# Integer phases, smaller first loads and other filler matmuls in the opening of an FFT and GeGLU kernel

## The chip, the cores and the metric

The kernel runs on one core of a Trainium2 chip. A core has five engines that run side by side, each with its own instruction queue: PE (matrix products, with PEld, its weight loads), DVE (vector work), ACT (activation functions and copies), POOL (general work) and SP, which here only issues DMA transfers. They meet through semaphores. The metric is the device time of one execution in microseconds; the median of a few runs counts.

## The reference

The input `x` has 8 batches of 3008 rows of 256 numbers. It is transformed by a Fourier transform along the rows and another along the columns, the real part is kept, and every one of the 24064 rows then goes through a gated feed-forward block with 1536 hidden units:

```
X = np.fft.fft(x, axis=1); X = np.fft.fft(X, axis=2); y = X.real
g = y @ w_gate;  gelu = 0.5 * g * (1 + erf(g / sqrt(2)))
out = (gelu * (y @ w_val)) @ w_out
```

All inputs and the output are fp32.

## The kernel before

The transform along the 3008 rows is split as 64 times 47. **Stage one** is the 64-point part: the rows of one batch are loaded into three tiles `xin` (8 rows of 256 for each of 128 partitions, line 201 `load_x`), folded into sums and differences of mirrored columns (`fold_x`, line 218; the two columns that have no partner are copied by `singles` on POOL), and multiplied by a table `G` of cosines and sines. For batch 0 this is done by `a_group` (line 513) in six groups J of four rows each: 16 small matmuls per group, copied from PSUM into the tile `S1`, and written from there by a DMA into the tile `Ap`, which has another order of partitions. **Stage two** is the 47-point part (`b_steps`, line 560): matmuls with `Ap` as weights and small tables `TP`, `TQ`, `T0P`, `T0Q`. The column transform is multiplied into the gate and value weights once (`gen_w`, with the table `CW`). What follows, the feed-forward block of all 8 batches in units of 512 columns, with the transforms of the next batch mixed in by a written plan, is nearly all of the time and is not edited.

The tables are made on the chip. `phase_g` (line 330) makes phases of `G` as products of a row number and a column number, for the first eight rows on DVE, for the next eight as eight ACT copies; adds a quarter turn for the cosines; and takes off whole turns with `reduce_phase`: two DVE operations, adding and subtracting a large constant `MAGIC` to round. `sin_g` then takes the sine on ACT, once for each sign of a column `col_h`, and `turn_g` derives eight more rows. `phase_c`, `reduce_c` and `sin_c` do the same for `CW`; `phase_t` and `sin_t` for the small tables, with `cols_t` and `quats` making columns for them.

The order on each engine is that of the program: every call is kept in program order, and the engines wait for one another only through the semaphores that the framework places from the tiles. DMAs are issued by SP in order, and each takes one of eight completion semaphores in turn ("lanes"); a DMA on a lane whose earlier user has not been seen to complete waits for it first. `warm(n)` (line 867) issues n matmuls of 512 columns whose result nobody reads: fillers. Their numbers are `WF = (10, 4)`: ten ahead of the first `gen_w` calls and four behind them, right before stage two; two more stand after the second group. In the profile nearly every instruction has line 25, a helper that records it, so tiles are what tells them apart; the tiles `dv` and `ev` hold the phases, since they share memory with later tiles of those names.

The part of the program around the change, before:

```
    for i in range(3):
        for a0, n in ((0, 8),) if i < 2 else ((0, 4), (4, 4)):
            fold_x(0, i, vec, a0, n, single=False)
    ...
    for J in range(6):
        a_group(J)
        if J == 1:
            warm(2)
    reduce_c()
    pt = phase_t()
    warm(WF[0])
```

Of the kernel before, what the change touches and what calls it, by code (L numbers as in the profile page):

```python
# [8 lines left out]

FP32 = mybir.dt.float32  # L10
BF16 = mybir.dt.bfloat16
AF = mybir.ActivationFunctionType
ALU = mybir.AluOpType

MAGIC = 12582912.0
TWO_PI = 2.0 * math.pi
# [11 lines left out]
def _sub(base: bass.AP, free_pattern, free_offset, part_start=0, part_num=None):  # L28
    p_step, p_count = base.ap[0]
    if part_num is None:  # L30
        part_num = p_count - part_start
    pat = [[p_step, part_num]] + [list(x) for x in free_pattern]
    off = base.offset + part_start * p_step + free_offset
    return ap_replace(base, ap=pat, offset=off)
# [3 lines left out]
def kernel(  # L38
# [24 lines left out]
    B, T, C = x.shape  # L63
# [27 lines left out]
    CW = const_pool.tile([128, NCH, 2, 128], BF16)  # L91
# [19 lines left out]
    col_a = const_pool.tile([128, 1], FP32)  # L111
    col_f = const_pool.tile([128, 1], FP32)
    col_b = const_pool.tile([128, 1], FP32)
    col_c = const_pool.tile([128, 1], FP32)
    col_j = const_pool.tile([128, 1], FP32)
    prow = const_pool.tile([1, 641], BF16)
    cols = const_pool.tile([128, 5], FP32)
# [58 lines left out]
    def apart(log, half, inst):  # L176
        for other, h in log:
            if half is not None and h is not None and h != half:
                tc.declare_no_dep(
                    getattr(inst, "ins", inst), getattr(other, "ins", other),  # L180
                    reason="the two halves of the tile are two banks")
        log.append((inst, half))
        return inst
# [16 lines left out]

    def load_x(b, i):
        xt = xins[i]
        for o, n, nh in ([(0, 7, 2), (7, 1, 1)] if i == 2 else [(0, 8, 2)]):
            src = ap_replace(
                x, ap=[[N2 * C, N1], [HJ * C, nh], [1, n * C]],
                offset=x.offset + (b * T + 8 * i + o) * C)
            p_step = xt[:, :, :].ap[0][0]
            dst = ap_replace(
                xt[:, :, :], ap=[[p_step * 2 // nh, N1 * nh], [1, n * C]],
                offset=xt[:, :, :].offset + o * C)  # L210
            sync.dma_start(out=dst, in_=src)
# [6 lines left out]
    def fold_x(b, i, eng, a0=0, an=8, single=True):  # L218
        xt = xins[i]
        o0 = (8 * i + a0) * C  # L220
        lo = _sub(xt, [[C, an], [1, 127]], a0 * C + 1)
        hi = _sub(xt, [[C, an], [-1, 127]], a0 * C + 255)
        ea = _sub(xf, [[C, an], [1, 127]], o0 + 1)
        od = _sub(xf, [[C, an], [1, 127]], o0 + 129)
        eng.tensor_tensor(ea, lo, hi, op=ALU.add)
        eng.tensor_tensor(od, lo, hi, op=ALU.subtract)
        if single:
            singles(i, a0, an)
# [10 lines left out]
    iota(rowj, [[15, HJ]], 0, 0)  # L239
    iota(_sub(rowk, [[1, 33]], 0), [[1, 33]], 0, 0)  # L240
    iota(_sub(rowk, [[1, 31]], 33), [[1, 31]], 1, 0)
    pool.tensor_scalar(rowk, rowk, 1.0 / 64.0, None, op0=ALU.mult)

    iota(_sub(rowc, [[128, 2], [1, 128]], 0), [[0, 2], [1, 128]], 0, 0)
    pool.memset(_sub(rowc, [[1, 1]], 128), 128.0)
# [25 lines left out]
    TG = TO + 2 * NJ  # L271

    def rows_t():
        pool.tensor_scalar(col_c, col_p, 1.0 / C, None, op0=ALU.mult)
        iota(_sub(rowt, [[N2, 2], [1, N2]], 0), [[0, 2], [1, N2]], 0, 0)
        iota(_sub(rowt, [[NJ, 2], [1, MID]], TO), [[0, 2], [1, MID]], 0, 0)
        iota(_sub(rowt, [[NJ, 2], [1, MID - 1]], TO + MID), [[0, 2], [1, MID - 1]], 1, 0)
        pool.memset(_sub(rowt, [[NJ, 2]], TO + NJ - 1), 0.0)
        pool.memset(_sub(quat, [[1, NJ]], TO), 0.25)
        pool.memset(_sub(quat, [[1, NJ]], TO + NJ), 0.0)  # L280
        iota(_sub(rowt, [[NG, 2], [1, NG]], TG), [[0, 2], [-11, NG]], 0, 0)
        pool.memset(_sub(quat, [[1, NG]], TG), 0.25)
        pool.memset(_sub(quat, [[1, NG]], TG + NG), 0.5)
# [28 lines left out]
    vec.scalar_tensor_tensor(col_a, col_f, -719.0, col_a, op0=ALU.mult, op1=ALU.add)  # L312
    vec.tensor_scalar(rowj, rowj, col_a, None, op0=ALU.add)
    vec.scalar_tensor_tensor(col_b, col_f, -2.0, col_p, op0=ALU.mult, op1=ALU.add)
    vec.tensor_scalar(col_h[1], col_b, -TWO_PI, None, op0=ALU.mult)
    vec.tensor_scalar(col_h[0], col_b, TWO_PI, -TWO_PI, op0=ALU.mult, op1=ALU.add)

    def reduce_phase(ph, tmp):
        vec.tensor_scalar(tmp, ph, MAGIC, None, op0=ALU.add)
        vec.scalar_tensor_tensor(tmp, tmp, MAGIC, ph, op0=ALU.subtract, op1=ALU.subtract)  # L320

    def red2_tile():
        return work.tile([128, 512], FP32, tag="glm", bufs=3, name="red2")
# [4 lines left out]
    reds = []  # L328

    def phase_g(i):  # L330
        ph, red = pha_g[i // 2][:, i % 2, :], red_g[i // 2][:, i % 2, :]
        reds.append(red)
        if i == 0:
            vec.tensor_tensor(
                _sub(ph, [[64, 8], [1, 64]], 0), _sub(rowj, [[1, 8], [0, 64]], 0),
                _sub(rowk, [[0, 8], [1, 64]], 0), op=ALU.mult)
        else:
            for k in range(8):
                act.activation(ph[:, 64 * k : 64 * k + 64], rowk[:, :], AF.Copy,
                               scale=rowj[:, 8 * i + k : 8 * i + k + 1])  # L340
        cos = _sub(ph, [[64, 8], [1, 33]], 0)
        vec.tensor_scalar(cos, cos, 0.25, None, op0=ALU.add)
        reduce_phase(ph, red)

    def sin_g(i):
        for h in range(2):
            act.activation(
                _sub(G, [[128, 8], [1, 64]], i * 8 * 128 + h * 64),
                _sub(reds[i], [[64, 8], [1, 64]], 0), AF.Sin, scale=col_h[h][:, :])

    def turn_g(odd):
        for to, of, n, sign in (((1, 33, 8, 1.0), (33, 1, 8, -1.0), (3, 35, 8, -1.0), (35, 3, 8, 1.0))
# [29 lines left out]
    redc = []  # L382

    def phase_c():
        both = red2_tile()
        redc.append(both)
        for q, (o, n) in enumerate(((0, 129), (129, 127))):
            act.activation(both[:, o : o + n], rowc[:, o : o + n], AF.Copy, scale=col_c[:, :],
                           bias=0.25 * (q + 1))

    def reduce_c():
        reduce_phase(redc[0][:, :C], redc[0][:, C : 2 * C])

    def sin_c():
        act.activation(_sub(CW, [[1, C]], 0), redc[0][:, C : 2 * C], AF.Sin, scale=-TWO_PI)
        for o, sign in ((0, 1.0), (1, -1.0)):
            act.activation(_sub(CW, [[2, 128]], C + o), _sub(CW, [[2, 128]], o), AF.Copy, scale=sign)

# [114 lines left out]
    def a_group(J):  # L513
        if "S1" not in st[0]:
            st[0]["S1"] = S1_tile()
        S1 = st[0]["S1"]
        if J % 4 < 2:
            ps, log = ps_v(), []
            both = ps
            banks = [(ps[:, h, :], log) for h in range(2)]  # L520
        else:
            banks = [(f(), []) for f in ((ps_g, ps_g) if J % 4 == 2 else (ps_o, ps_d))]
        for gq in range(4):
            for jl in range(4):
                jj = 4 * J + jl
                ps, log = banks[gq // 2]
                apart(log, gq // 2, pe.matmul(
                    _sub(ps, [[1, C]], gq % 2 * C, 32 * jl, 32),
                    _sub(G, [[32, 4], [4, 8]], (jj - 16 * (J > 3 and gq % 2 == 0)) * 128 + gq),
                    _sub(xf, [[1, C]], jj * C), start=True, stop=True))  # L530
        if J > 3:
            for o, n, scale in ((0, 2, 1.0), (2, 1, -1.0), (3, 1, 1.0)):
                ps, log = banks[o // 2]
                to, of = _sub(S1, [[1, n * C]], (4 * J + o) * C), _sub(ps, [[1, n * C]], o % 2 * C)
                apart(log, o // 2, vec.tensor_scalar(to, of, scale, None, op0=ALU.mult) if J == 4 and o else
                      act.activation(to, of, AF.Copy, scale=scale))
        if J < 2:
            act.activation(_sub(S1, [[1, 4 * C]], 4 * J * C), both, AF.Copy)
        for h in range(2 * (J in (2, 3))):
            dst = _sub(S1, [[1, 2 * C]], (4 * J + 2 * h) * C)  # L540
            act.activation(dst, banks[h][0], AF.Copy)
        p_step = Ap[:, :, :].ap[0][0]
        sync.dma_start(
            out=ap_replace(
                Ap[:, :, :], ap=[[6 * p_step, 16], [1, NG * C]],
                offset=Ap[:, :, :].offset + (J % 2 * 3 + J // 2) * p_step),
            in_=_sub(S1, [[1, 4 * C]], 4 * J * C))
# [314 lines left out]
        return steps  # L862


    WF = (10, 4)

    def warm(n, w=None):
        ps = ps_d()
# [8 lines left out]
    sin_g(0)  # L877
    sin_g(1)
    turn_g(True)
    phase_c()  # L880
    for i in range(3):
        for a0, n in ((0, 8),) if i < 2 else ((0, 4), (4, 4)):
            fold_x(0, i, vec, a0, n, single=False)
        if i == 0:
            singles(0)
            cols_t()
            singles(1)
            quats()
            singles(2)
    for J in range(6):  # L890
        a_group(J)
        if J == 1:
            warm(2)
    reduce_c()
    pt = phase_t()
    warm(WF[0])
    for f0, n in ((256, 256), (512, 512)):
        for i in (1, 0):
# [206 lines left out]
```

## Time and profile before

| | us |
|---|---|
| median of 3 runs (lowest, highest) | 615.92 (615.8, 619.26) |
| the profiled execution's own time | 616.09 |
| its span, first to last instruction | 614.2 |
| PE busy | 595.6 (97%) |
| DVE busy | 567.1 (92%) |
| POOL busy | 501.7 (82%) |
| ACT busy | 487.2 (79%) |
| first matmul of stage one | 8.97 |
| last copy into `S1` ends | 16.03 |
| first matmul of stage two | 21.08 |

Times inside a run count from the span's first instruction. A timeline line gives the start, the length from the first to the last of the merged instructions, engine, line, operation, what it writes and reads, the size, how many, and in brackets how long the engine was idle before it and who ended that. A line of waits gives who waited for whom, then total, times and longest. A line of the chain gives start, length and what the end of the run was waiting for at that moment, followed back from the last instruction.

### The profile page before, as it was taken

Reading aid. Unit: us, or ns where it says so; the run is one execution under the profiler, and the core shown is the slowest. Engines: PE = TensorE matmul, PEld = TensorE weight load, DVE = VectorE, ACT = ScalarE, POOL = GpSimd, SP = SyncE. Lnnn points to the kernel's source line nnn. Section 1 sums busy time; section 2 is a strip of 40 time slices with the busy share of each in tenths; the row PEclk is TensorE's granted clock in tenths of the full one; section 3 lists DMA queues with packets and bytes.
Section 4 is the critical chain, followed back from the end, with each engine's and each line's share of the span. In section 5 each row is a group of like instructions: output and inputs, shape, how many; then the busy total and the mean of one; then the engine's idle time right before and its main releaser. Section 6 shows DMA issues by size and latency. Waiting matters only on the chain.

```text
span 614.2 us, 13086 instructions
## 1 busy us (share of the span) xinstructions
PE 595.6 (97%) x4572; PEld 398.5 (65%) x4629; DVE 567.1 (92%) x689; ACT 487.2 (79%) x1011; POOL 501.7 (82%) x525
## 2 busy tenths in 40 slices
PE   4899999999999999999999999999999999999997
PEld 2456666666676666666667666766667666666666
DVE  8688999999999999999999999999999999999992
ACT  8798789877898787977789778887789878776762
POOL 5599999989999899798998899898997755665552
PEclk9999999999999999999999999999999999999999
DMA  7999423762257613673246633477123712222123
GB/s 277 340 241 268 132 69 112 204 215 60 61 149 196 197 40 80 193 225 113 65 120 172 194 92 74 121 207 214 41 73 94 203 37 55 55 47 52 39 48 87
DMA packets 63460, 80.79 MB, mean 132 GB/s; under 512 B 8187, under 2 KB 56827, under 8 KB 60675
## 3 DMA queue, kind: packets, MB, share of 16 engines
q1 hardware_dynamic: 61682, 79.05, 45.3%
q0 software_dynamic: 1552, 0.79, 0.9%
q8 instruction: 36, 0.59, 0.4%
q14 instruction: 30, 0.24, 0.1%
q10 hardware_dynamic: 160, 0.13, 0.1%
HBM read 43.47 MB, written 35.68 MB: 129 GB/s over the span
## 4 chain that ended last, share of the span: by engine, by line
PE 90%; ACT 4%; DMA 3%; DVE 1%; issue 1%; SPq 1%; ACTq 0%; POOL 0%
PE ps_o L25 37%; PE ps_g L25 27%; PE ps_v L25 19%; PE ps_d L25 6%; ACT S L25 2%; DMA out_dram<-osb 1%; DMA xin<-in_x_dram 1%; ACT osb L25 1%; ACT glm L25 1%; DMA Ap<-S 1%; SPq L850 1%; ACT glp L25 0%; DVE h L25 0%; DVE ev L25 0%; DVE dv L25 0%
## 5 line engine op out<-in xcount | busy, mean ns | idle before, releaser
L25 POOL TENSOR_TENSOR h<-glm,dv 128x1024 bf16<-128x1024 bf16 (+1 forms) x138 | 291.0, 2111 | 80.1 <-DVE dv L25 59.5
L25 PE MATMUL ps_o<-Wo_sb,h 128*128 128x256 bf16 x2124 | 284.2, 273 | 1.0
L25 PEld LDWEIGHTS <-h 128*128 128x128 bf16 x2208 | 210.9, 97 | 58.4 <-issue 0.9
L25 DVE SCALAR_TENSOR_TENSOR ev<-nq,WN,ps_v 128x512 f32<-128x512 bf16 (+1 forms) x276 | 202.0, 733 | 23.4 <-PE ps_v L25 15.0
L25 ACT ACTIVATE glp<-ps_g 128x512 bf16<-128x512 f32 (+1 forms) x288 | 169.8, 589 | 37.2 <-PE ps_v L25 18.6
L25 ACT ACTIVATE glm<-ps_g 128x512 bf16<-128x512 f32 (+1 forms) x241 | 142.2, 590 | 56.6 <-PE ps_g L25 44.0
L25 DVE TENSOR_TENSOR h<-glp,ps_v 128x1024 bf16<-128x1024 bf16 (+2 forms) x150 | 172.9, 1153 | 4.2 <-ACT glp L25 3.5
L25 DVE SCALAR_TENSOR_TENSOR dv<-ev,ps_v 128x1024 f32<-128x1024 f32 (+1 forms) x138 | 164.7, 1194 | 0.0
L25 POOL TENSOR_TENSOR xf<-xin 128x254 bf16<-128x254 f32 x168 | 118.4, 727 | 0.4 <-DMA xin<-in_x_dram 0.4
L25 PE MATMUL ps_v<-Y,WOP 128*128 128x512 bf16 (+1 forms) x288 | 107.8, 374 | 0.1
L25 PE MATMUL ps_v<-Y,WE 128*128 128x512 bf16 (+1 forms) x286 | 107.3, 375 | 0.0
L25 PE MATMUL ps_g<-Y,WE 128*128 128x512 bf16 (+1 forms) x266 | 99.4, 374 | 0.0
L25 PE MATMUL ps_g<-Y,WOP 128*128 128x512 bf16 (+1 forms) x257 | 96.1, 374 | 0.8
L25 PE MATMUL ps_g<-Y,WOM 128*128 128x512 bf16 (+1 forms) x241 | 90.4, 375 | 0.2
L25 PEld LDWEIGHTS <-WOP 128*128 128x128 bf16 x576 | 55.5, 97 | 49.2 <-ACT WOP L25 0.6
L25 PEld LDWEIGHTS <-WE 128*128 128x128 bf16 x576 | 56.0, 97 | 27.9 <-issue 2.2
L25 ACT ACTIVATE osb<-ps_o 128x512 f32<-128x512 f32 x92 | 54.2, 589 | 13.4 <-PE ps_o L25 12.4
L25 POOL TENSOR_TENSOR go<-go,ge 128x480 f32<-128x480 f32 (+1 forms) x47 | 58.1, 1236 | 7.1 <-DVE go L25 7.1
L25 PEld LDWEIGHTS <-Ap 96*128 96x128 bf16 (+1 forms) x561 | 39.5, 96 | 34.0 <-issue 2.6
L25 ACT ACTIVATE S<-ps_d 128x512 bf16<-128x512 f32 x82 | 48.9, 596 | 0.2 <-PE ps_d L25 0.2
L25 PEld LDWEIGHTS <-G 128*128 128x128 bf16 (+1 forms) x280 | 21.0, 109 | 25.4 <-issue 5.0
L25 DVE SCALAR_TENSOR_TENSOR go<-nq,WN,ps_g 128x480 f32<-128x480 bf16 (+1 forms) x47 | 34.3, 730 | 2.6 <-ACT glp L25 1.9
(134 smaller groups left out, 370.2 us busy)
## 6 DMA issues: line engine op xcount, KB each, us to landing
out_dram<-osb SPq DMA_DIRECT2D x358, 64.0 KB
xin<-in_x_dram SPq DMA_DIRECT2D x16, 1024.0 KB
Ap<-z SPq DMA_DIRECT2D x20, 512.0 KB
xin<-in_x_dram SPq DMA_DIRECT2D x8, 896.0 KB
z<-S SPq DMA_DIRECT2D x7, 768.0 KB
z<-S SPq DMA_DIRECT2D x6, 512.0 KB
nq<-nrow SPq DMA_DIRECT2D x8, 376.2 KB
z<-S SPq DMA_DIRECT2D x9, 256.0 KB
```

Of the source, the lines that this page charges most:

```text
L25: return lambda *a, **k: self._tc.keep_in_program_order(call(*a, **k))
L850: queues[q % 2].dma_start(out=rows_ap(rows[0][0], 32, rows[1][0] - rows[0][0], 2), in_=_sub(t, [[C, 2], [1, C]], 0, 32 * q, 32))
```

## The change

Four things change, all ahead of stage two of batch 0.

The phases of `G` and `CW` are made as integers: the product of the two numbers is kept unscaled (the two POOL operations that scaled by 1/64 and 1/256 go), the quarter turn is 16 of 64 or 64 of 256, and whole turns are taken off by one AND with 63 or 255. The sines get a scale with the division in it and a bias column (`col_o`, `col_i`), so that their arguments lie about zero. The small tables keep `reduce_phase`.

`load_x` loads batch 0 in pieces of four rows, seven DMAs instead of four. Folding, `singles` and `a_group` go piece by piece in one loop; `cols_t` comes after the first piece, `phase_c` after the second group, `quats` ahead of the last piece but one's group, `reduce_c` and `phase_t` ahead of the last group.

The copies of group 4 out of PSUM that DVE made go to ACT (the condition `J == 9` is never true).

The fillers: one after each of the first three groups, then eight and nine instead of ten and four.

```diff
@@ load_x
-        for o, n, nh in ([(0, 7, 2), (7, 1, 1)] if i == 2 else [(0, 8, 2)]):
+        ends = [(7, 1, 1)] if i == 2 else []
+        parts = [(0, 4, 2), (4, 4 - len(ends), 2)] if b == 0 else [(0, 8 - len(ends), 2)]
+        for o, n, nh in parts + ends:
@@
-    pool.tensor_scalar(rowk, rowk, 1.0 / 64.0, None, op0=ALU.mult)
...
-        pool.tensor_scalar(col_c, col_p, 1.0 / C, None, op0=ALU.mult)
...
-    vec.tensor_scalar(col_h[1], col_b, -TWO_PI, None, op0=ALU.mult)
-    vec.tensor_scalar(col_h[0], col_b, TWO_PI, -TWO_PI, op0=ALU.mult, op1=ALU.add)
+    for t, s in ((col_h, -TWO_PI / 64.0), (col_o, math.pi)):
+        vec.tensor_scalar(t[1], col_b, s, None, op0=ALU.mult)
+        vec.tensor_scalar(t[0], col_b, -s, s, op0=ALU.mult, op1=ALU.add)
+    vec.memset(col_i, math.pi)
@@ phase_g
-        ph, red = pha_g[i // 2][:, i % 2, :], red_g[i // 2][:, i % 2, :]
+        ph, red = (t[i // 2][:, i % 2, :].bitcast(INT32) for t in (pha_g, red_g))
...
-        vec.tensor_scalar(cos, cos, 0.25, None, op0=ALU.add)
-        reduce_phase(ph, red)
+        vec.tensor_scalar(cos, cos, 16.0, None, op0=ALU.add)
+        vec.tensor_scalar(red, ph, 63, None, op0=ALU.bitwise_and)
@@ sin_g
-                _sub(reds[i], [[64, 8], [1, 64]], 0), AF.Sin, scale=col_h[h][:, :])
+                _sub(reds[i], [[64, 8], [1, 64]], 0), AF.Sin, scale=col_h[h][:, :], bias=col_o[h][:, :])
@@ phase_c, reduce_c, sin_c
-            act.activation(both[:, o : o + n], rowc[:, o : o + n], AF.Copy, scale=col_c[:, :],
-                           bias=0.25 * (q + 1))
+            act.activation(both[:, o : o + n], rowc[:, o : o + n], AF.Copy, scale=col_p[:, :],
+                           bias=64.0 * (q + 1))
...
-        reduce_phase(redc[0][:, :C], redc[0][:, C : 2 * C])
+        vec.tensor_scalar(redc[0][:, C : 2 * C], redc[0][:, :C], 255, None, op0=ALU.bitwise_and)
...
-        act.activation(_sub(CW, [[1, C]], 0), redc[0][:, C : 2 * C], AF.Sin, scale=-TWO_PI)
+        act.activation(_sub(CW, [[1, C]], 0), redc[0][:, C : 2 * C], AF.Sin,
+                       scale=-TWO_PI / C, bias=col_i[:, :])
@@ a_group
-                apart(log, o // 2, vec.tensor_scalar(to, of, scale, None, op0=ALU.mult) if J == 4 and o else
+                apart(log, o // 2, vec.tensor_scalar(to, of, scale, None, op0=ALU.mult) if J == 9 else
@@
-    WF = (10, 4)
+    WF = (8, 9)
@@
-    phase_c()
-    for i in range(3):
-        for a0, n in ((0, 8),) if i < 2 else ((0, 4), (4, 4)):
-            fold_x(0, i, vec, a0, n, single=False)
-        if i == 0:
-            singles(0)
+    for J in range(6):
+        fold_x(0, J // 2, vec, J % 2 * 4, 4, single=False)
+        singles(J // 2, J % 2 * 4, 4)
+        if J == 0:
             cols_t()
-            singles(1)
+        if J == 4:
             quats()
-            singles(2)
-    for J in range(6):
+        if J == 5:
+            reduce_c()
+            pt = phase_t()
         a_group(J)
         if J == 1:
-            warm(2)
-    reduce_c()
-    pt = phase_t()
+            phase_c()
+        if J < 3:
+            warm(1)
     warm(WF[0])
```

## The prediction

> **What bounds the kernel now.** I read the engine table first, then the chain that ended last, then PE's own waits, then the opening instruction by instruction. The table and the slices, of the page of before:
>
> ```profile
> PE 595.6 (97%) x4572; PEld 398.5 (65%) x4629; DVE 567.1 (92%) x689; ACT 487.2 (79%) x1011; POOL 501.7 (82%) x525
> ...
> PE   4899999999999999999999999999999999999997
> ```
>
> PE is full except in the first two slices (15.4 us each) and the last. PE's waits, all of them:
>
> ```profile
> PE ps_o L25 <- POOL prow L25: 4.8, 1, 4.8
> PE ps_v L25 <- POOL xf L25: 3.9, 1, 3.9
> PE ps_v L25 <- DMA Ap<-S: 2.1, 1, 2.1
> PE ps_d L25 <- DVE WOM L25: 0.3, 1, 0.3
> PE ps_g L25 <- DVE wb L25: 0.2, 1, 0.2
> ```
>
> After stage two begins (21.08 us) PE waits 0.3 us more in the whole span; from there to 607.8 us it is busy 583.3 of 586.7 us. So this change, which edits only what stands ahead of stage two, can move the end only by moving the start of stage two. The chain of that stretch, start and length:
>
> ```profile
> 1.47 7.11 DMA xin<-in_x_dram
> ...
> 12.44 3.60 ACT S L25 x8
> 16.03 0.03 ACT CW L25
> 16.06 4.67 DMA Ap<-S
> 20.73 0.35 issue
> 21.08 0.36 PE ps_v L25 x8
> ```
>
> Stage two waits for the sixth Ap write, that for ACT's last copy into S. The engines there, from the timeline (start, length):
>
> ```profile
> 4.37 0.69 DVE L25 SCALAR_TENSOR_TENSOR dv<-dv,ev 128x512 f32<-128x512 f32 x1
> 5.10 1.33 ACT L25 ACTIVATE G<-dv,col_h 128x512 bf16<-128x512 f32 x2 [0.74 <-DVE dv L25]
> 6.47 2.35 DVE L25 TENSOR_TENSOR xf<-xin 128x1016 bf16<-128x1016 f32 x2
> 9.06 4.77 DVE L25 TENSOR_TENSOR xf<-xin 128x1016 bf16<-128x1016 f32 x6
> 10.80 1.03 PE L25 MATMUL ps_d<-G 128*128 128x512 bf16 x2
> 14.36 1.68 ACT L25 ACTIVATE S<-ps_v 128x512 bf16<-128x512 f32 x4
> 14.55 2.32 PE L25 MATMUL ps_d<-G 128*128 128x512 bf16 x9
> 17.96 1.03 PE L25 MATMUL ps_d<-G 128*128 128x512 bf16 x4
> ```
>
> DVE has no gap from 0.85 to 13.83: phases until 6.5, then folds. All of x has landed at 11.0 (completions of the four loads: 6.11, 8.57, 10.80, 11.01, so 2.46 us per MB), so DVE, not the load, holds the last fold. The fillers show the clock: the first two start 0.40 apart, those from 14.55 on 0.215 apart. The granted-clock column reads 1.00 throughout, yet the matmuls halve their spacing at 13.4 us, after 4.4 us of dense work.
>
> **Part 1, integer phases.** Each reduction loses its second DVE operation: the steps from it to the next are 4.37 to 4.98 and 5.86 to 6.47, 0.61 each, so 1.22 goes. Two more small columns and a memset come in front, 0.06 to 0.07 each by the col_h pair: +0.18. The AND stands where the MAGIC add stood. No row shows an integer AND; it lies between the fp32 scalar operation on 512 elements (0.50) and the two-input one (0.69). I take 0.50, the row of the same form; the other end adds 0.4 on DVE. Integer output of ACT's eight phase copies: no row; the fp32 copies take 0.33, and 0.02 more each (a twelfth, taken as the bound either way) would be covered, since the next DVE operation begins at 4.55 against their end at 4.37. POOL loses 0.37 and 0.55 (rowk, col_c); nobody waits for either. So folding can begin at 6.47 - 1.22 + 0.18 = 5.4, and sin_g at 4.56 instead of 5.10.
>
> sin_g and sin_c get a bias column. The Trainium skill, "ScalarE: Activation LUTs", section "What ACT_TABLE_LOAD costs", says that each column operand adds about 93 ns to an activation. Rows: Sin with a scale column took 0.358 us at 94 elements and 0.706 at 512; Sin with constant scale took 0.490 at 256, on the same line (0.28 + 0.833 ns an element). A column more cost nothing there, so I take 0. By that rule of the Trainium skill the four would add 0.37, an estimate, and the forecast would be 615.2.
>
> **Part 2, pieces of four rows.** Seven x loads instead of four: SP issues at 0.6 to 0.7 each end near 5.4 instead of 3.4, and two weight loads queue behind; those landed at 11.74 and 12.43 and are read at 16.6, so 2 us is covered. Lanes are reused three loads earlier: the second weight load waits for the first x piece, long landed. The pieces land each 1.23 us from 4.9 to 11.0. Half-size loads have no row: between the MB load (2.46 us, 426 GB/s) and the 256 KB weight load (0.69 us, 380 GB/s). At the slow end the last lands at 11.9, which delays the last fold by 0.2. I take the fast end.
>
> Folds: a 4x127 operation steps by 0.60 (11.35, 11.96, 12.56, 13.16). Twelve take 7.2, with cols_t (0.32) after the first pair: pairs start at 5.4, 6.9, 8.1, 9.3, 10.5, 11.7, end 13.0, each after its piece. Before: 13.83. POOL's quats (1.4) now stand between singles 4 and 5: 10.4 to 11.8, then 0.4; still before 13.0.
>
> ACT, by steps between its own starts (Sin 0.63, the four turns 1.06, a 1024 copy 0.92, 512 0.48, 256 0.26, phase_c 0.54): sin_g 4.56 to 7.06, turns to 8.13, J0 at 8.13 (PE began it at 6.7, a cold group takes 0.86 and its drain), J1 at 9.3 (its fold ends 8.2), phase_c, moved behind J1, 10.2, J2 10.75, J3 11.7, J4 12.65. J4's two 256 copies leave DVE (0.76) and cost ACT 0.53; J5 at 13.65 and done at 14.85. Before: 16.03. Gain on S **1.18**. ACT is the bound, with 0.2 to spare over DVE: either DVE bound above costs at most that much beyond it.
>
> SP issues J5's Ap write at 14.9. In what time it lands is the large unknown. Before, latencies from issue to landing grew: 3.18, 3.53, 4.10, 4.21, 4.30, 4.67. By the last, 19.55. By throughput: from 15.5 to 18.5 us the queue began 356 packets of 2 KB, 119 per us, so 1.08 us for one write's 128; J0's data cannot pass the two weight loads, whose packets run to about 12, so it lands near 14.3 as before, and five more make 19.7. Both ends of the latency are kept, 3.2 (18.1) and 20.7; I take 19.65, so stage two at 20.0 instead of 21.08: **-1.08**.
>
> **Part 3, fillers.** One cold filler (0.43) after each of J0, J1, J2: PE is then 1.29 of each 1.2 us, hidden by ACT. Eight after J5: 13.6 to 15.4 warm; gen_w needs CW (Sin at 14.65, turns to 15.7) and ends near 16.5; nine fillers, 1.94, end 18.5, before Ap. Cost 0, as long as Ap lands after 18.5; gain 0, since the 2.1 us hole of before ran no matmul slower after it (0.18 us each for 47 columns).
>
> **Sum.** Nothing else moves; the weight loads of 256 and 512 columns follow J5 on SP and come as much earlier. Profiled run 616.09 (span 614.2 and 1.9 around it) - 1.08 = 615.0. The median shown is 615.92, 0.17 lower: **614.8**.
>
> **Rivals.**
> A, the DMA queue keeps its old end: the writes start behind the weight loads at 12 in both kernels, and the skew of the 16 engines (J5's completions ran from 19.37 to 20.73) eats the earlier issue. For: the queue was never idle long, only some 100 packets (0.8 us) were lost between 12 and 15.5. Against: those are just what earlier issue fills. Landing 20.3 to 20.7: 615.5 to 616.0. Chance 0.2.
> B, the last write meets an emptier queue, as J0 did: 14.9 + 3.2 = 18.1, then the nine fillers are last, until 18.6: stage two at 18.7, **613.5**. For: issues are 1.0 to 1.5 apart, a write takes 1.08. Against: the weight loads in front. 0.13.
> C, **slower: the fillers run cold.** Pieces leave holes in PE (after J3, no filler, 0.86 of 1.2), so the clock may not have risen by 13.6. Eight fillers at 0.43 end 17.0, gen_w cold (8 x 0.21) 18.7, nine more 22.6: stage two 1.5 late, and up to half of another 4.4 us lost: 617.4 to 619.6. It decides only if the clock is still low at 18.7; from 13.6 on PE would be dense, longer than the 4.4 us that sufficed. Chance 0.1. The Trainium skill, "TensorE: Matmul & The Clock Gate", Part 1, has the clock rise after a free-running window of 3.4 us of activity; by that it is up by 17 at the latest and C gives nothing. The rise at 13.4 agrees.
>
> Forecast 0.55, own range 614.2 to 615.5; 0.02 for the rest. The range of **613.4 to 617.0** takes in A, B and the bounds (0.4 for DVE and loads) and leaves out C. One per cent (6.2 us) is about what a measurement of this kernel can tell from no change; even stage two at 17, hardly possible with x landing at 11, is 4 us: faster by over 1% 0.02, slower 0.03, within 0.95.
>
> **What would show it.** First fold near 5.4; S ends near 14.9; sixth Ap write issued then, landing 19.4 to 20; fillers end before it; stage two at 20.0; from there to the end 593 us as before. Wrong if the AND takes 0.7, if PE's fillers still step 0.43 after 14, or if the stretch after stage two changes its length.

## The result and the profile after

| | before | after |
|---|---|---|
| median of 20 runs each, same chip (us) | 617.14 | 619.64 |
| lowest to highest | 615.79 to 619.44 | 616.15 to 623.3 |
| ratio after / before, 95% interval | | 1.0036 [1.002, 1.0051] |
| profiled execution, its span | 616.09, 614.2 | 619.41, 617.6 |
| mean granted clock of that execution | 1.000 | 0.994 |
| last copy into `S` ends (us from the span's start) | 16.03 | 15.06 |
| sixth `Ap` write: issued, landed | 16.06, 20.73 | 15.08, 21.84 |
| first matmul of stage two | 21.08 | 21.98 |
| from there to the end of the span | 593.2 | 595.6 |

The forecast was 614.8, within 613.4 to 617.0. The kernel became slower by about a third of a per cent, less than the one per cent that the chances call a difference, but outside the range and on the other side of no change. (The ratios, here and below, are those on record with their intervals; they are not the quotients of two medians, which would be 1.0041 here.)

The engine table and two rows of the 40 slices, from the page of the kernel after:

```profile
PE 599.5 (97%) x4576; PEld 400.2 (65%) x4633; DVE 565.0 (91%) x691; ACT 488.4 (79%) x1013; POOL 503.5 (82%) x526
...
PE   5899999999999999999999999999999999999997
...
PEclk9799999999999999999999999999999999999999
```

PE is busy 3.9 us longer (595.6 before) with 4 matmuls more, and the clock row has a 7 in its second slice, 15.4 to 30.9 us. PE's waits of the kernel after, in total, times, longest:

```profile
PE ps_o L26 <- POOL prow L26: 4.5, 1, 4.5
PE ps_v L26 <- DMA Ap<-S: 3.0, 1, 3.0
PE ps_v L26 <- POOL xf L26: 2.5, 2, 1.8
PE ps_v L26 <- DVE xf L26: 0.4, 1, 0.4
PE ps_d L26 <- DVE WOM L26: 0.3, 1, 0.3
```

The wait for `Ap` has grown from 2.1 to 3.0. The chain of the same kernel (start, length, what the end waited for at that moment):

```profile
3.40 7.30 DMA xin<-in_x_dram
10.75 0.74 POOL xf L26
...
12.78 0.61 POOL xf L26
13.45 0.44 PE ps_v L26 x8
13.91 1.15 ACT S L26 x3
15.08 6.76 DMA Ap<-S
21.84 0.14 issue
21.98 0.48 PE ps_v L26 x8
```

All up to 15.08 is an improvement: `S` is done 0.97 earlier. The next line takes it back. The write that took 4.67 us takes 6.76. Then the timeline of PE, still after (start, length, operation, size, number; in brackets PE's idle time before it):

```profile
16.86 2.11 PE L26 MATMUL ps_d<-G 128*128 128x512 bf16 x9
21.98 0.48 PE L26 MATMUL ps_v<-TP,Ap 96*128 96x47 bf16 x8 [3.01 <-DMA Ap<-S]
...
26.07 0.58 PE L26 MATMUL ps_v<-Y,WE 128*128 128x481 bf16 x1
26.45 0.61 PE L26 MATMUL ps_g<-Y,WE 128*128 128x481 bf16 x1
...
28.54 0.37 PE L26 MATMUL ps_v<-Y,WOP 128*128 128x481 bf16 x1
28.75 0.37 PE L26 MATMUL ps_g<-Y,WE 128*128 128x481 bf16 x1
```

The nine fillers step by 0.215, so PE is at full clock until they end. After the hole a 481-column matmul takes 0.6 us and steps by 0.40; from 28.2 on it takes 0.37 and steps by 0.21. Between them lies a stretch at half clock. Cut into the windows in which the trace's clock record changes (the columns are the window, its length, busy time and number of instructions of each engine, then the granted clock, the DMA engines' share and their rate):

```profile
core 0: us, PE busy (x) PEld busy (x) DVE busy (x) ACT busy (x) POOL busy (x), PEclk, DMA share, GB/s
...
14.49:17.91 3.42, 3.36 (x19) 1.74 (x19) 2.36 (x8) 3.37 (x11) 1.32 (x4) 1.00 1.08 247
17.91:21.32 3.41, 1.05 (x5) 0.29 (x3) 0.00 (x0) 0.62 (x2) 0.00 (x0) 1.00 1.08 248
21.32:24.73 3.41, 2.75 (x68) 2.72 (x69) 1.41 (x6) 1.11 (x4) 1.37 (x3) 0.50 1.06 396
24.73:28.15 3.42, 3.42 (x40) 2.08 (x40) 1.46 (x7) 1.79 (x6) 3.12 (x3) 0.50 1.01 399
28.15:31.56 3.41, 3.41 (x21) 1.82 (x20) 2.27 (x5) 3.09 (x8) 3.06 (x5) 1.00 1.04 408
```

The clock record of this run reads 1.0 for 10.24 us, 0.5 for 6.83, then 1.0 for 590.51: multiples of 3.413 us. In the window from 17.91 PE worked 1.05 of 3.41 us, and the next two were granted half. The same windows of the kernel before, in the run that the prediction was made from:

```profile
16.78:20.19 3.41, 1.99 (x13) 1.07 (x11) 2.07 (x7) 2.61 (x7) 1.32 (x4) 1.00 0.95 238
20.19:23.60 3.41, 2.52 (x96) 2.51 (x97) 1.41 (x6) 1.39 (x5) 1.22 (x2) 1.00 1.02 339
23.60:27.02 3.42, 3.40 (x29) 1.78 (x25) 2.57 (x9) 3.04 (x10) 1.99 (x2) 1.00 1.03 416
```

There the 2.1 us hole was cut by a window's edge, and neither part emptied a window. So the 3.4 us between the two spans are: stage two starts 0.89 later; stage two itself, to the first matmul on `Y`, takes 4.10 instead of 2.68, 1.42; and from there to the end 591.55 instead of 590.48, 1.07. The 1.42 is the clock, and so is most of the 1.07: 0.80 of it is there by 35 us, behind the two slow windows. The other 0.27 come later and at full clock (ACT begins its writes to `glm` 3.11 us later than in the kernel before from 35 to 277 us, and 3.26 later from 309 us on). So the clock explains 2.2 of the 3.4; what the 0.27 are is not known.

The mean clock of every other run tells how much was lost without a trace, though not where in the run. One cold window (3.41 us at half the clock) lowers the mean over 617 us by 0.0028, two by 0.0055. The end of the span takes a little more: behind PE's last matmul the record falls to 0.5 again, in the traces for up to the last 2.3 us (e12), at most 0.0019. So the runs form three groups: 0.998 to 1.000, 0.995 to 0.997, 0.993 to 0.994. I call them held, one window, two windows. (Two whole windows give 0.9945 or less at these lengths, so the three runs at 0.995 count as one window and a long end.) Of the 20 runs of the kernel after 3 held, 4 lost one window and 13 lost two (median 620.5; the held ones 617.02). Of 35 runs of the kernel before in the first set of experiments 15 held (616.09), 17 lost one, 3 lost two. So the kernel before had the same illness in more than half of its runs, and its one profiled execution did not.

### The profile page after: what moved, and what is told of

Its sections match the earlier page's. It is cut to its first block, busy times and chain, and to the rows that moved or that the text cites. A ratio compares the mean times of both kernels' runs of the same rounds, so it can differ in the third digit from the quotient of the medians.

```text
span 617.6 us, 13107 instructions
## 1 busy us (share of the span) xinstructions
PE 599.5 (97%) x4576; PEld 400.2 (65%) x4633; DVE 565.0 (91%) x691; ACT 488.4 (79%) x1013; POOL 503.5 (82%) x526
## 4 chain that ended last, share of the span: by engine, by line
PE 89%; DMA 3%; ACT 3%; DVE 1%; SPq 1%; issue 1%; POOL 0%; ACTq 0%; DVEq 0%
PE ps_o L26 37%; PE ps_g L26 27%; PE ps_v L26 19%; PE ps_d L26 6%; DMA xin<-in_x_dram 1%; ACT S L26 1%; DMA Ap<-S 1%; DMA out_dram<-osb 1%; ACT glm L26 1%; ACT osb L26 1%; SPq L855 1%; SPq L26 0%; ACT glp L26 0%; DVE h L26 0%; POOL xf L26 0%
## 5 line engine op out<-in xcount | busy, mean ns | idle before, releaser
L26 PEld LDWEIGHTS <-Ap 96*128 96x128 bf16 (+1 forms) x561 | 40.9, 99 | 35.0 <-issue 3.5
L26 PEld LDWEIGHTS <-G 128*128 128x128 bf16 (+1 forms) x284 | 20.7, 105 | 26.1 <-ACT S L26 1.9
```

Of the source, the lines that this page charges most:

```text
L26: return lambda *a, **k: self._tc.keep_in_program_order(call(*a, **k))
```

## The experiments

The theory to be tested: the pieces of `x` delay the queue, so `Ap` lands later; PE's longer hole then lets the clock drop. The rivals: it is the earlier and denser issue of the `Ap` writes that delays them, or the integer phases cost the time, or the clock drops for another reason than the hole. All runs are timed beside the kernel before on the same chip. Ratios are to it, with 95% intervals. The landing times come from the completion records of one profiled execution of each.

| kernel | last `x` | sixth `Ap` write | stage two | median (lowest to highest) | clock: held / one / two windows | ratio |
|---|---|---|---|---|---|---|
| before | 11.01 | 16.06 to 20.73 | 21.08 | 617.07 (615.72 to 619.36) | 15 / 17 / 3 | |
| after | 11.90 | 15.08 to 21.84 | 21.98 | 619.64 (616.15 to 623.3) | 3 / 4 / 13 | 1.0036 [1.002, 1.0051] |
| e1 whole loads | 11.08 | 15.87 to 20.00 | 20.44 | 616.10 (615.69 to 616.26) | 12 / 0 / 0 | 0.9984 [0.9972, 0.9995] |
| e2 24 fillers | 12.91 | 16.30 to 23.47 | 23.60 | 618.35 (617.38 to 619.17) | 11 / 1 / 0 | 1.0018 [1.0005, 1.0031] |
| e3 pieces alone | 12.18 | 17.23 to 22.95 | 23.09 | 617.08 (616.3 to 619.73) | 6 / 5 / 1 | 1.0005 [0.9989, 1.002] |
| e4 before, 13 fillers | 11.00 | 16.06 to 21.03 | 21.43 | 616.22 (615.8 to 616.83) | 12 / 0 / 0 | 0.9984 [0.997, 0.9997] |
| e5 64 partitions | 17.45 | 21.87 to 26.23 | 26.86 | 622.98 (622.8 to 623.18) | 5 / 0 / 0 | 1.0088 [1.0066, 1.0109] |
| e6 e1, no second fillers | 10.99 | 15.85 to 19.73 | 20.03 | 618.18 (616.87 to 618.62) | 0 / 1 / 10 | 1.0005 [0.9991, 1.0019] |
| e7 integers alone | 11.31 | 16.27 to 20.70 | 21.06 | 617.14 (615.41 to 618.26) | 1 / 7 / 3 | 0.9997 [0.9982, 1.0012] |
| e8 16 fillers | 13.58 | 16.94 to 23.94 | 24.08 | 618.69 (616.56 to 621.12) | 8 / 2 / 2 | 1.0018 [1.0, 1.0035] |
| e9 even, odd | 12.38 | 16.94 to 21.39 | 21.52 | 617.01 (616.29 to 618.83) | 7 / 3 / 0 | 0.9997 [0.998, 1.0013] |
| e10 first tile only | 12.21 | 16.69 to 21.61 | 21.85 | 617.81 (617.06 to 620.52) | 8 / 0 / 2 | 1.0007 [0.9989, 1.0024] |
| e11 seven and one | 11.89 | 15.75 to 21.37 | 21.51 | 617.40 (616.6 to 621.63) | 6 / 3 / 1 | 1.0013 [0.999, 1.0036] |
| e12 six queued | 12.39 | 16.66 to 21.35 | 22.30 | 618.40 (617.03 to 621.9) | 3 / 3 / 4 | 1.0031 [1.0009, 1.0054] |
| e13 eight queued | 11.00 | 15.74 to 21.05 | 21.19 | 616.29 (615.89 to 617.1) | 10 / 0 / 0 | 0.9987 [0.9971, 1.0004] |

The kernel before had medians of 617.07, 617.29, 617.28 and 617.38 in the four sets (e1 to e4, e5 to e8, e9 to e11, e12 and e13), and held, lost one and lost two windows in 15 / 17 / 3, 9 / 13 / 6, 11 / 9 / 5 and 6 / 10 / 3 runs. One trace stands behind each landing time. The kernel after, e2 and e8 load `x` alike, and there its last piece came at 11.90, 12.91 and 13.58; so of two kernels with cut loads it can't be said which is later. The six with whole loads lie at 10.99 to 11.31.

**e1: the kernel after, with the whole loads of before.**

```diff
-        ends = [(7, 1, 1)] if i == 2 else []
-        parts = [(0, 4, 2), (4, 4 - len(ends), 2)] if b == 0 else [(0, 8 - len(ends), 2)]
-        for o, n, nh in parts + ends:
+        for o, n, nh in ([(0, 7, 2), (7, 1, 1)] if i == 2 else [(0, 8, 2)]):
```

> The changed kernel with batch 0 loaded by the four DMAs of before (8, 8, 7 and 1 rows); folding, groups, integer phases and fillers stay in pieces as changed. Theory 1, the smaller x transfers slow the queue and everything behind them: x lands at 11.0 instead of 11.9 us, the first Ap write near 14.3 instead of 15.0, the sixth between 19.8 and 20.6 instead of 21.84, stage two starts 20.2 to 20.9, PE's hole ahead of it shrinks from 3.2 to under 2.1 us, and the clock stays full in most runs: median 615 to 617. Theory 2, the earlier and denser Ap issues crowd each other and the x pieces have no part in it: the sixth write still lands after 21.3, the hole stays about 3 us and the median stays at 619 to 620.

`x` is in at 11.08 again, the sixth `Ap` write lands at 20.00, and the wait for `Ap` all but goes. That alone does not rule out the early issue, since only the first write is issued nearly as early as in the kernel after (9.75 against 9.35; 11.14 before), and the sixth 0.8 later. The table speaks for the loads, as far as single traces can: in the six kernels with whole loads the sixth write lands at 19.73 to 21.05, in all with `x` in more loads at 21.35 or later, also where it is issued late, as in e3 (17.23). PE's first waits in e1:

```profile
PE ps_o L26 <- POOL prow L26: 4.5, 1, 4.5
PE ps_v L26 <- POOL xf L26: 2.8, 1, 2.8
PE ps_v L26 <- DMA Ap<-S: 0.7, 1, 0.7
```

All 12 runs hold the clock and lie within 0.6 us. The load in pieces is what costs the kernel after its 3.5 us; without it the rest of the change beats both kernels, the one before by little: 0.9984 [0.9972, 0.9995]. That gain is the clock's, as far as the times tell: e1's median of 616.10 equals that of the held runs of the kernel before, 616.09, and e4 below reaches the same ratio by fillers alone.

**e2: the kernel after, 24 fillers instead of nine.**

```diff
-    WF = (8, 9)
+    WF = (8, 24)
```

> The changed kernel with 24 fillers instead of 9 behind gen_w, so that PE has matmuls from 16.9 to about 22.0 us. Theory 1, the clock drops because PE has a hole of about 3 us ahead of stage two: no drop in any run, granted clock 1.000, stage two takes 4.0 instead of 6.1 us, stage two still starts at 22.0 to 22.2; median 616.8 to 617.5, and the spread of runs shrinks to about 1 us. Theory 2, the loss is the later Ap write alone and the clock costs nothing: the median stays at 619 or more.

The clock holds in 11 of 12 runs, and 1.3 us of the median goes. But the median, 618.35, and the spread, 1.8, miss the expectation (616.8 to 617.5, about 1 us). In this trace `Ap` landed at 23.47 and the fillers end at 23.5, so in a run whose `Ap` lands earlier they would themselves be what stage two waits for. e8 has fewer.

**e3: the kernel before with the pieces alone** (`load_x` of after, all else of before).

> The kernel before with one edit, batch 0 loaded in the seven pieces of the change; folds and all else as before. Theory 1, the pieces slow the queue: last x lands near 11.9 us instead of 11.0, Ap's sixth write lands 0.5 to 1.2 later than 20.73, PE's hole grows to about 3 us and the clock drops in most runs: median 618 to 620, slower than before. Theory 2, pieces cost nothing: the sixth write at 20.7 and the median at 617.

In the profile the pieces alone do what they do in the kernel after: last `x` at 12.18, sixth `Ap` write at 22.95, a hole of 3.4 us, one cold window. The median of 617.08 is a miss of the expectation: it equals that of the kernel before. Its held runs are 0.4 slower (616.5 against 616.09), but not more of them drop than of the kernel before's. So the delay is seen in one execution and is at best weak in the median; why it weighs less here than in the kernel after, no run tells.

**e4: the kernel before with 13 fillers instead of four.**

```diff
-    WF = (10, 4)
+    WF = (10, 13)
```

> The kernel before with 13 fillers instead of 4 behind gen_w, up to about 20.8 us. Theory 1, the slow half of the runs of before (616.7 to 619.4 against 615.8) are runs in which a clock window fell on its 2.1 us hole: with the hole filled all runs come within 0.5 us of 615.9, clock 1.000. Theory 2, the spread of before has another cause (transfers, the later stages): it stays, with a median near 617.

This tests the clock alone: nothing else is touched, and stage two starts no earlier (21.43). The spread of 3.6 us shrinks to 1.0 (the highest run, 616.83, lies outside the expected half microsecond), all 12 runs hold, the ratio is 0.9984 [0.997, 0.9997]. Two windows of e4, with PE now filled ahead of `Ap`:

```profile
16.21:19.62 3.41, 3.41 (x21) 1.77 (x19) 2.36 (x8) 3.15 (x9) 1.33 (x4) 1.00 0.99 247
19.62:23.03 3.41, 2.69 (x70) 1.93 (x68) 0.97 (x5) 1.00 (x4) 1.22 (x2) 1.00 1.07 365
```

Nine fillers of no use are worth as much here as e1 with all its other edits.

**e6: e1 without its nine second fillers**, the opposite dose.

```diff
-    WF = (8, 9)
+    WF = (8, 0)
```

> The changed kernel with whole loads of x, and without the nine fillers behind the first gen_w calls. With whole loads PE waited 0.7 us for Ap; without the nine (9 by 0.215) the hole is about 2.6 us. Theory 1, a hole of this size lets the granted clock drop at the start of stage two in those runs where the hole fills most of a clock window: a mean clock of 0.997 or less in at least a third of the runs, those runs 1.5 to 4 us longer, median 616.8 to 619, spread 3 us and more. Theory 2, the hole costs nothing beyond the wait (the prediction's reading): median 615.9 to 616.3 as with the nine, spread under 0.8 us.

Stage two starts at 20.03, the earliest of all, and yet the median is 618.18, 2.1 more than e1, and no run holds the clock. The windows:

```profile
15.81:19.22 3.41, 1.67 (x11) 0.70 (x8) 1.42 (x4) 3.35 (x10) 1.31 (x4) 1.00 0.89 254
19.22:22.63 3.41, 2.60 (x66) 2.63 (x66) 1.41 (x6) 1.18 (x5) 1.22 (x2) 0.50 0.80 251
22.63:26.05 3.42, 3.42 (x43) 2.08 (x40) 1.46 (x7) 1.64 (x6) 1.82 (x2) 0.50 1.04 399
```

So the nine fillers hide nothing of the wait and are worth 1.3 to 2.1 us (by the ratios and by the medians, since e1 and e6 were timed in different sets) by what the clock does after them. The prediction's reading that the fillers neither cost nor gain anything is refuted.

**e7: the kernel before with the integer phases alone** (loads, folds and fillers of before).

> The kernel before with the integer phases alone: loads, order of the folds and fillers (10 and 4) as before. Theory 1, folds can start only when the first whole load of x is there (6.1 us), so the integer phases give at most 0.4 us on the last copy into S (15.6 to 16.0 instead of 16.03), the sixth Ap write lands at 20.3 to 20.8, the hole ahead of stage two stays near 2 us, and the median (616.5 to 617.3) and the spread (3 us) are those of the kernel before. Theory 2, the integer phases are the part that costs time (the bias column makes each Sin 0.08 longer, four of them 0.3): S ends at 16.1 to 16.4 and the median is 617.4 or more.

`S` ends at 15.98 instead of 16.03, `Ap` lands at 20.70 instead of 20.73, and the median is that of the kernel before: 0.9997 [0.9982, 1.0012]. With whole loads the first fold can't begin before the tile is in, at 6.1 to 6.4 us, so nearly all of the 1.1 us that the phases give DVE goes unused. This part neither helps nor harms.

**e8: the kernel after with 16 fillers.**

```diff
-    WF = (8, 9)
+    WF = (8, 16)
```

> The changed kernel with 16 fillers instead of nine behind the first gen_w calls: 7 more, 1.5 us, so they end near 20.3, ahead of any landing of the sixth Ap write seen in the changed kernel (21.1 and later), and 1.5 us of PE's 3.2 us hole is filled. Theory 1, the changed kernel lost its time in two parts, the later landing (0 to 2 us from run to run) and the clock drop (2 to 3 us): the drop goes in nearly all runs (mean clock 0.998 and more), the later landing stays, median 616.6 to 618.0, none above 619. Theory 2, the clock drop comes from something else than the hole: as the changed kernel, 619 to 620, with a clock of 0.993 to 0.995 in most runs.

Half a hit. Held runs rise from 3 of 20 to 8 of 12, with a median of 617.68, in the expected 616.6 to 618.0. But four runs still lost one or two windows, and the median of all, 618.69, and the highest, 621.12, are above the expectation. The delay varies more than expected: in this profile `x` came at 13.58 and `Ap` at 23.94. So more fillers cannot make up for the pieces: the held runs are still 1.6 us behind e1.

**e5, e9, e11: seven loads of the same bytes, cut another way.** In e5 each load fills 64 adjacent partitions with 8 KB rows; in e9 the even or the odd partitions; in e11 seven rows and one row.

```diff
 # e5
...
+            for a0, an in ((0, 32), (32, 32)) if b == 0 and nh == 2 else ((0, N1),):
...
 # e9
...
+            for h in range(2) if b == 0 and nh == 2 else (None,):
...
 # e11
-        parts = [(0, 4, 2), (4, 4 - len(ends), 2)] if b == 0 else [(0, 8 - len(ends), 2)]
+        parts = [(0, 7 - len(ends), 2), (7 - len(ends), 1, 2)] if b == 0 else [(0, 8 - len(ends), 2)]
```

> The changed kernel with batch 0's x still in seven loads of the same bytes, but cut by partitions (64 of 128) instead of by rows, so that a packet is 8 KB or 7 KB as before the change. Theory 1, the 4 KB packets let the 16 DMA engines drift apart: x lands as with whole loads, the last at 11.0 to 11.2 us, the skew between a load's first and last completion stays near 0.5, the sixth Ap write lands at 19.8 to 20.7, stage two starts by 20.9, median 615.8 to 616.5. Theory 2, it is the number of loads ahead of the Ap writes (nine instead of six), whatever their packets: last x at 11.7 to 12.2, skew 0.7 and more, the sixth Ap write at 21.3 or later, median 617.5 to 619.5.

> The changed kernel with batch 0's x in seven loads of the same bytes, cut into even and odd partitions, so that packets are 8 and 7 KB as before the change and every load reaches over the whole width of the tile (the cut into two halves of 64 adjacent partitions ran at half the rate: 8 KB packets at about 600 ns instead of 309, x at 17.45 us). Theory 1, the 4 KB packets are what puts the 16 DMA engines out of step: packets at 309 ns, the last x at 11.0 to 11.3, sixth Ap write at 19.8 to 20.8, median 615.8 to 616.5. Theory 2, seven loads instead of four do it: packets stretched, last x at 11.7 or later, median 617.5 and more. If packets take 600 ns again, the run tells nothing between the two, but that partitions and not bytes set the rate.

> The changed kernel with seven x loads, but cut seven rows and one row (six, one and the single one for the last tile): most bytes in 7 KB packets, the rest in 1 KB packets, all 128 partitions in each load. Theory 1, half-size packets of 4 KB are what hurts: the last x at 11.0 to 11.4, sixth Ap write at 19.8 to 20.9, median 615.8 to 616.8. Theory 2, more loads in the queue put the engines out of step whatever the packets: last x at 11.7 or later, skew of a load's completions over 0.7, median 617.5 and more.

e5 decided nothing between its theories, as it ran into something else: the 8 KB packets took about 600 ns instead of 309, and `x` needed until 17.45. The DMA rates of e5 in 40 slices of 0.55 us from 0 to 22 us:

```profile
GB/s 0 0 0 60 149 283 268 223 238 238 238 179 209 194 268 194 179 238 238 223 218 210 222 222 222 183 274 199 160 184 266 354 359 283 242 220 231 268 209 179
```

Some 220 GB/s where whole loads move 430. The Trainium skill, "SBUF — State Buffer", section "Door 1: The DMA port swizzle", says that the rate goes by how many of 16 ports the partitions reach, and that adding 64 to a partition's number changes the port; by that, 64 adjacent partitions reach half of them, and half the rate is what e5 shows.

e9 and e11 decide it: with packets of 8, 7 and 6 KB, over the whole width of the tile, `x` lands as late (12.38, 11.89) as with 4 KB packets, and the sixth write too (21.39, 21.37). The size of the packets is not the cause. The medians, 617.01 and 617.40, lie between the two theories and decide nothing.

**e10: pieces in the first tile only. e12: the same, with one weight load moved behind the first `Ap` write. e13: whole loads, but each of the two weight loads split in two.** They ask whether it is the `x` loads or the number of transfers queued at the start, which is six in before, e1, e4, e6 and e7, and seven or more in all the other kernels up to here.

```diff
 # e10
+        parts = [(0, 4, 2), (4, 4 - len(ends), 2)] if b == 0 and i == 0 else [(0, 8 - len(ends), 2)]
 # e12: e10, and
-    for i in (1, 0):
-        load_w(0, i, 256)
+    load_w(0, 1, 256)
...
+        if J == 0:
+            load_w(0, 0, 256)
 # e13: e1, and
-        load_w(0, i, 256)
+        load_w(0, i, 128)
+        load_w(128, i, 128)
```

> The changed kernel with pieces of four rows for the first of the three tiles alone, the other two whole (five x loads instead of seven, a third of the bytes in 4 KB packets). Theory 1, the harm grows with the 4 KB packets: in between, last x at 11.0 to 11.6, sixth Ap write at 20 to 21.2, median 616.0 to 617.5. Theory 2, the first pieces alone do it, since the stretched packets in the traces lie at 5 to 6 us, inside the second and third piece: as with all pieces, last x at 11.7 or later, sixth Ap write at 21.3 or later, median 618 and more.

> As the kernel with pieces in the first tile alone (five x loads), but the second of the two weight loads goes to the queue behind the first Ap write, so that six transfers stand in the queue while x comes in, as before the change, instead of seven. In every kernel with six, x came in without a stretched packet after 6 us (last x 11.0 to 11.3); in every one with seven or more, packets were stretched from 5 us on (last x 11.7 to 13.6). Theory 3, the seventh transfer in the queue is the cause: no stretched packet after 6 us, last x at 11.0 to 11.3, and, the queue being ahead, median 615.5 to 616.6. Theory 2, more than four x loads are the cause: last x at 11.7 to 12.3 as with pieces in the first tile before, median 617 to 618.5.

> The changed kernel with whole loads of x (four), but each of the two weight loads in the opening split into two of half the columns, so that eight transfers are queued while x comes in, none of them a piece of x. Theory 3, transfers in the queue beyond the sixth stretch the packets, whatever they carry: 8 KB packets over 330 ns after 6 us, last x at 11.5 to 13, sixth Ap write at 21 or later, median 617 to 620. Theory 2, only x in more than four loads does: packets at 309 ns, last x at 11.0 to 11.2, sixth Ap write by 20.8, median 615.8 to 616.8.

e10 with a single cut is late as well (`x` at 12.21, the sixth write at 21.61), so one cut is enough; its median, 617.81, lies between the theories. e12 has six transfers queued and `x` is late (12.39). Its later times say less: in its trace the clock fell inside stage one, from 12.97 to 19.80, so its first eight fillers took 3.5 us instead of 1.7, and stage two waited for the fillers (22.30) and not for `Ap` (21.35). e13 has eight and `x` is on time (11.00), it held in all 10 runs, and its median is 616.29; but its sixth write, at 21.05, is the latest with whole loads, as theory 3 expected, and 2.36 us lie between its first and its last engine (2.46 in the kernel after, 1.36 before). So for the late `x` the number of transfers falls as a cause, and what remains is `x` in more than four loads; for the spread of the writes it does not fall. The DMA rates in the same slices of before, after, e10 and e13, in this order:

```profile
GB/s 0 0 0 45 164 149 402 447 417 417 417 447 417 432 412 430 417 430 304 385 354 69 82 179 305 268 186 168 246 246 246 257 250 160 177 309 292 320 339 331
```

```profile
GB/s 0 0 0 0 119 209 417 410 417 365 194 320 395 402 380 365 410 384 417 384 376 376 376 227 216 227 227 253 231 242 238 287 205 227 216 214 253 287 343 367
```

```profile
GB/s 0 0 0 22 119 216 365 447 402 439 358 328 357 387 264 389 436 417 387 345 367 391 356 231 190 190 201 250 138 238 242 246 250 197 220 331 201 203 259 333
```

```profile
GB/s 0 0 0 30 194 149 387 447 357 432 432 462 402 372 436 417 417 419 340 342 324 319 253 235 212 227 223 238 201 264 223 246 201 300 290 285 305 277 317 318
```

With a cut the rate falls after 5.5 us, to 194 in one slice (after, the eleventh) and to 328 and again to 264 (e10, the twelfth and fifteenth); without one it stays, from 5 to 9.9 us, at 412 and more (before) or 372 and more (e13). In the records single packets are stretched in the kernels with a cut, up to 1.48 us for 4 KB instead of 0.16 (e2; 1.19 in the kernel after). In all eight (e5 aside) most of it begins at 5.1 to 5.6 us; with whole loads no packet of `x` that starts after 3.5 us takes over 1.6 times its usual length. Summed over the 16 engines from 3.4 us on, the packets of `x` took 4.8 to 14.6 us beyond their usual length (e5 aside), against 0.4 to 1.2 in the kernels with whole loads. What in the queue stretches them is open: no run here shows it.

## Why the prediction was wrong

**Part 1, integer phases.** Right in its result: folds were forecast to begin at 5.4 and begin at 5.195; the AND took 0.49 and 0.43 (forecast 0.50). Wrong in one term: "a column more cost nothing there, so I take 0". The four sines of `G` after:

```profile
4.33 2.92 ACT L26 ACTIVATE G<-dv,col_o,col_h 128x512 bf16<-128x512 int32 x4
```

One takes 0.807 instead of 0.706 and steps by 0.705 instead of 0.63: 0.30 for four. By the rule of the Trainium skill ("ScalarE: Activation LUTs", "What ACT_TABLE_LOAD costs": about 93 ns for each column operand) it would be 0.37, and the trace agrees with it, not with my comparison of rows of different lengths. It cost nothing at the end, since the sines started 0.23 earlier than forecast.

**Part 2, `S` done at 14.85.** Measured 15.06. The step mis-sized is "I take the fast end" for the landing of `x`: the last piece landed at 11.90, the slow end (11.9), and the 0.2 that was put against it is what `S` lost. `quats` and the last copies by POOL, forecast to end before 13.0, ended at 13.38, beside a fold that ended at 13.30: no more than 0.1 of its own.

**Part 2, the landing of the sixth write, "I take 19.65".** This is the step that failed. It was issued at 15.08, 0.2 after the forecast, and landed at 21.84, beyond even the slow end of 20.7. The working took the queue as one server with a rate, from 119 packets of 2 KB a microsecond. The rate held nearly: 623 such packets began from 13.0 to 18.5, 113 a microsecond (629 in the same stretch before). The first completions of the six writes, from 13.92 to 19.38, followed each other by 1.09, as forecast (1.08). What did not hold is that 16 engines finish together. The second weight load landed at 13.87 instead of 12.43, the first write at 15.03 instead of the 14.3 that was assumed "as before". The first engine completed the sixth write at 19.38 (19.37 before), the last at 21.84 (20.73). The landing is that of the slowest engine, and the spread was 1.36 before and 2.46 after. I had half of it in rival A, in which the skew of the 16 engines "eats the earlier issue", at a chance of 0.2, but with the skew of before. It was larger in e3, with the pieces (2.43), and not in e1, without them (1.27). How the spread gets from `x` to the writes is not shown: in e2 and e8 every write has 2.6 us of it or more, in the kernel after the first four have 1.0 to 1.2 and only the fifth 2.44, and e13 has 2.36 without a cut. The bounds of the unknown latency, 18.1 to 20.7, were both from the kernel before, and nothing in them could show a queue out of step.

**Part 3, "gain 0, since the 2.1 us hole of before ran no matmul slower after it".** This failed too, and is the dearer one: 2.2 of the 3.4 us between the two profiled runs. The observation was right, of one execution. Over the runs of the kernel before, 20 of 35 lost a window or two. The spread of the three times given, 615.8 to 619.26, which the prediction did not explain, fits it: two cold windows came to 619.2 in the later runs. A longer hole then turned a frequent small loss into a regular large one. One slip did no harm: "1.29 of each 1.2 us" is more than fits, and a cold group with its filler took PE 1.52, but ACT still began the copies of J2 at 10.77 (forecast 10.75).

**The rivals.** B fell with the landing. C, fillers at half clock, did not occur: the clock rose at 11.08, and the fillers step by 0.215. ("Up by 17 at the latest" counts one window from 13.6; a free-running window of 3.41 us may begin up to 3.41 later, so 20.4 was the bound.) Its 617.4 to 619.6 was nearly met by another way. The prediction named the sign that would refute it, "if the stretch after stage two changes its length": 595.6 against 593.2.

On the clock, the Trainium skill, "TensorE: Matmul & The Clock Gate", section "Why this matters for your kernels", advises against gaps of PE over about 3 us. The 3.0 us hole of the kernel after agrees with it. e6 and e7, with holes of 2.26 us in their traces, dropped as well, in every run of e6 and in 10 of 11 of e7; so the measurement is stricter than the rule.

## What to carry to other kernels

A hole of PE costs more than its length: ask what it does to the clock behind it, and judge that by the mean clock of all runs, not by one trace; nine useless matmuls ahead of a late transfer were worth 1.3 to 2.1 us here. A transfer lands when its slowest of 16 engines does, so cutting the loads at the head of a queue can delay the last write at its end even when rate and issue look right. Before believing that an earlier issue gains, look at the first and the last completion of the transfers, not only at the median or the rate.

## What the runs showed of the hardware that I had not expected

- The grant of PE's clock changes in steps of 3.413 us, and a run's mean clock shows how many of them were cold. A drop followed windows in which PE was busy for 1.05 us (after), 1.44 (e3), 1.67 (e6), 1.72 (e7) and 1.74 (e12, in stage one); windows with 1.85 (e13), 1.90 (e3) and 1.99 (before) were not followed by one. One case does not fit: e11 kept the clock after a window with 1.57. So about half of a window is where it turns, and no sharper value follows from these runs.
- Once it had dropped, one full window (e3, e7) or two (after, e6, e12) ran at half clock; in the two, the first had PE busy 2.75, 2.60 and 2.61 of 3.41 us.
- Loads of 512 KB into 64 adjacent partitions moved at half the rate (packets of about 600 ns, e5), into the 64 even or odd ones at nearly the full one (309 ns and some stretched, e9).
- POOL's copies of 8 numbers for each of 128 partitions took 0.32 and 0.24 us for the first two pieces of the kernel after, and 0.74 for the three that began within 0.03 us of a fold on DVE. That is shown by their times only; no run separated the two.
